# A forgetting-attention and bilinear feed-forward kernel: all operations in a new order around an early first feed-forward piece, reciprocals merged, one more batch masked by GpSimd, fewer idle matmuls

## The chip, the cores and the metric

The kernel runs on one core of a Trainium2 chip. The metric is device time in microseconds (us) of one execution; a kernel's time is the median over its runs. Before the change the median of 3 runs is 394.45 us, from 394.08 to 394.82 us.

TensorE (PE in the profile) does the matmuls, VectorE (DVE), ScalarE (ACT) and GpSimd (POOL) the elementwise work, and SyncE (SP) issues most DMA transfers. Each engine works through its own instructions in the order in which they were written out and waits on semaphores for the others.

## The reference

Eight batches of eight heads, 576 positions, head size 64. The scores carry a decay that is a difference of running sums of log f, the softmax is causal, and a feed-forward layer without a nonlinearity follows: the product of two projections, projected back.

```python
scores = np.matmul(q, k.transpose(0, 1, 3, 2)) / np.sqrt(64)
cum    = np.cumsum(np.log(np.clip(f, 0.0001, 1.0)), axis=-1)
scores = np.where(causal, -1e9, scores + cum[:, :, :, None] - cum[:, :, None, :])
attn   = softmax(scores)                                # row maximum, exp, row sum, division
x      = np.matmul(attn, v).transpose(0, 2, 1, 3).reshape(4608, 512)
out    = ((x @ w_a) * (x @ w_b)) @ w_out                # 512 -> 1536 -> 512
```

## The kernel before, in words

**Attention.** The work is cut into 32 *pairs* t = 4 b + pr: batch b and two of its heads. The 576 queries of a pair make five row blocks i = 0 to 4 (the last has 64 rows), and block i sees the key blocks 0 to i. Per pair, in groups of blocks (1 and 0; 2; 3; 4): `qk_group` or `qk_first` makes the scores in PSUM (operations `qk t.g`, L538, L550); DVE finds the row maxima (`max t.i`, L645, or L673, where the decay is added in the same pass); ACT takes exp with the row sum beside it (`exp t.i`, L700 and L704); DVE takes the reciprocal of the sums (L712 and L714, one per pair and block); POOL scales the rows (`norm t.i`, L725; in batches 0 and 1 partly ACT, L723). The blocks 0 to 2 make part A of the probabilities, 3 and 4 part B. They are transposed, by a DMA of SP's queue (`tr`, L739), in batch 0 and in part of batch 1 by PE (`ptr`, tile psP) with an eviction (`pev`). PE then multiplies with v (`pv`, L768 and L783), and DVE or ACT writes the result into xT (`ev`).

**Masks and decay.** In batch 0 PE adds decay and causal mask to the scores by small matmuls (crow with pick, neg64 with low). In batch 1 (pairs 4 to 7, the set PSPREAD) the decay rows are spread over the partitions by PE (`bm`, tile scd) and evicted (`bc`), and PE still adds the mask. From batch 2 on (the set MASKP, pairs 8 to 31) the decay rows come by DMA, and POOL makes a masked copy of them (`mc`, L630, and `ml`, L637), so that DVE's pass over the scores adds decay and mask together.

**Feed-forward.** The tokens are cut into pieces of 256, 256, 256, 384, 512, 512, 512, 512 and 384, and the last 1024 are done by a Strassen-Winograd scheme (tiles wg, wb, og, ob, om). A piece multiplies with w_a (`psa`), ACT copies it (`acopy`), multiplies with w_b (`psb`), DVE multiplies both (`mul`), and `pso` projects back. A piece can start when `ev` of all four pairs has written its tokens: the first 256 tokens need only blocks 0 and 1 of the pairs 0 to 3. The weights come by DMAs that POOL issues (`ldw`, L509, six `wa`/`wb` pieces ahead of most others): the first 512 columns of w_a and of w_b in two halves each, the other 1024 in two halves each, then w_out in three.

**Idle matmuls.** `wake` (L74, tile wake) multiplies the identity with itself in the start; nothing reads the result. There are 24 such operations of four matmuls.

**The order.** Nothing is scheduled when the kernel is built. Every operation has a number in the order of its construction; ORDER lists all 2480 numbers, CHOICE gives the engine of each operation that may run on several, and SLOTS gives the buffer that each tile takes, in turn. The instructions of each engine, and of the DMA queues that it issues, stand in the sequence of that list.

Of the kernel before, what the change touches and what calls it, by code (L numbers as in the profile page):

```python
# [25 lines left out]
def kernel(  # L26
# [11 lines left out]
    nc = tc.nc  # L38

    B, H, S, D = q.shape  # L40
# [5 lines left out]
    NP = H // 2  # L46
# [58 lines left out]
    def paddings():  # L105
# [36 lines left out]
        PA:012302310231023102310231023102310231;PB:01101010101010101010101010101010;S:0101101001101001101010110  # L142
        0110101010101001010101010101010010011010100101001000100010011011010011010100110101001101010110101010101
        ;a16:0120120120120120120120120120120121021021201201201201021021020210210120120121021021021021021;bc:012
        0120120120120120120120120120;ff:01230123013200031230120131312313102312022101012133203012301230123012301
        2301302132021021230230201230231021301230123012012302131231231021230130230132103120301010312013210321023
        1023023102310321321302130213013210321032103102132132012312312303021021023103120313201302130230123120312
        0302102012120102301310210213023123201321301321320120320312032130213021302301213021303210312303021021320
        130213201302312031203120321032102301;ht:0123456789abcd0123456789abcd0123456789ab01cd2345678a019b23cd456
        8017a29bd345c0168279a34bd015c2;n16:01101001011000101001010101010101;n32:0120102102102102010202121220120  # L150
        110102121101202201201201202120;nv:0101010101;osb:010101010100101010101010101001;qd:01010101010101010101
        0101;sc:01010101010101010101010110100101011000101010110010010101101010101011010101010101010100101011101
        10010101011001010111010101010101010101010101010101;st:01234510324510324510324510324510
# [102 lines left out]
    for lo, hi in ((0, 256), (256, S)):  # L256
        n = hi - lo
# [257 lines left out]
    MASKP = {t for t in range(8, NP * B)}  # L515
# [28 lines left out]
    def qk_group(t, g):  # L544
# [7 lines left out]
        if g == 3 and t in MASKP:  # L552
# [156 lines left out]
    def do_recip(t, i):  # L709
        st = T[("st", t)]  # L710
        if i == 4:
            nc.vector.reciprocal(out=st[:, 28:29], in_=st[:, 18:19])  # L712
        else:
            nc.vector.reciprocal(out=st[:, 20 + 2 * i:22 + 2 * i], in_=st[:, 10 + 2 * i:12 + 2 * i])  # L714
# [106 lines left out]
    def attention(t, base):  # L821
# [75 lines left out]
        direct_ex = {}  # L897
        for g, gi in [(g, groups[g]) for g in ((0, 1, 3, 2) if t in MASKP else (0, 1, 2, 3))]:
            qk, su = qk_of[g], None
            for i in gi:  # L900
# [55 lines left out]
                rc = Op("DVE", 0.16, lambda _, i=i: do_recip(t, i), es, prio=prio(g))  # L956
                st_users.extend(es + [rc])
                for h in range(1 if i == 4 else 2):
                    nm = Op(None, {"POOL": NORM[i]} | ({"ACT": 0.2 + 0.00082 * 128 * (i + 1)} if b in EARLY else {}), lambda e, i=i, h=h: do_norm(e, t, i, h), [rc], prio=prio(g),
                            name=f"norm{t}.{i}")  # L960
                    st_users.append(nm)
                    pu[part].append(nm)
                    norms.setdefault(part, []).append(nm)
                    norm_of.append((i, nm))
# [593 lines left out]
    for n in cuts:  # L1558
# [5 lines left out]
        0 1 29 30 46 2 52 62 5 3 31 37 32 38 33-36 39 40 42 41 53 47 58 4 43 267 262 279 6-9 54 48 10 56 50 44  # L1564
# [161 lines left out]
```

## Time and profile before

| | |
|---|---|
| median of 3 runs | 394.45 us |
| profiled execution, its own time from first to last instruction | 394.4 us |
| PE busy | 381.1 us (97%) |
| DVE busy | 329.1 us (83%) |
| ACT busy | 299.4 us (76%) |
| POOL busy | 281.0 us (71%) |
| granted TensorE clock | 0.999 of full speed |

A row of a timeline has start and length in us, engine, line, operation, output and inputs, shapes, the number of instructions merged into it, and in brackets the idle time ahead and what ended it. A matmul's length contains its way through the array, so consecutive rows overlap; what a matmul takes from the stream is read from start to start. In a table of windows each engine has busy us and, in brackets, instructions.

### The profile page before, as it was taken

What the parts mean: (1) busy time and instruction counts of PE and PEld (TensorE: products, weight loads), DVE (VectorE), ACT (ScalarE), POOL (GpSimd) and SP (SyncE); (2) the same over time, 40 slices, a digit from 0 to 9 for tenths busy, and PEclk for the clock granted to TensorE, in tenths of its full rate; (3) what the DMA queues carried; (4) which work ended last, traced back from release to release, by engine and by line L of the source; (5) the groups of instructions that cost most, each with busy time, mean ns of one, the idle gap of its engine ahead of it and who ended that gap; (6) DMA issues with size and microseconds to landing.
All of it is one profiled execution on the core that took longest, in us unless ns stands there. A gap on an engine that the chain in (4) does not pass through costs nothing.

```text
span 394.4 us, 14909 instructions
## 1 busy us (share of the span) xinstructions
PE 381.1 (97%) x5816; PEld 253.9 (64%) x5816; DVE 329.1 (83%) x1035; ACT 299.4 (76%) x826; POOL 281.0 (71%) x482
## 2 busy tenths in 40 slices
PE   7899999999998999999899999999999999999996
PEld 3557887968765665655555655555555667666796
DVE  7888898998996888788788888757898899987992
ACT  4998999999886878868888588779899672556331
POOL 8689686768867689874899769578976891267600
PEclk9999999999999999999999999999999999999999
DMA  7999999999999999999998999999998898100005
GB/s 121 251 202 170 144 154 223 228 278 275 208 222 215 220 282 247 281 187 277 260 237 255 262 207 229 206 244 263 226 226 195 169 182 178 55 1 2 2 2 214
DMA packets 147190, 76.88 MB, mean 195 GB/s; under 512 B 124336, under 2 KB 128176, under 8 KB 147120
## 3 DMA queue, kind: packets, MB, share of 16 engines
q1 hardware_dynamic: 132824, 68.79, 77.9%
q0 software_dynamic: 14256, 7.08, 14.7%
q8 instruction: 45, 0.74, 0.8%
q14 instruction: 25, 0.20, 0.2%
q10 hardware_dynamic: 40, 0.07, 0.1%
HBM read 52.05 MB, written 9.58 MB: 156 GB/s over the span
## 4 chain that ended last, share of the span: by engine, by line
PE 73%; DMA 11%; DVE 5%; POOL 4%; ACT 3%; issue 2%; ACTq 0%; DVEq 0%; POOLq 0%
PE psa L74 15%; PE psb L74 15%; PE pso L74 13%; PE wg L74 5%; DMA PTA<-PA 5%; PE wb L74 4%; PE sc L550 3%; PE og L74 3%; DMA PTB<-PB 3%; PE pvx L768 3%; PE psT L358 2%; DVE S L673 2%; DMA wb<-in_moe_w_b_dram 2%; POOL PA L725 2%; PE wake L74 2%
## 5 line engine op out<-in xcount | busy, mean ns | idle before, releaser
L673 DVE CUSTOM_DVE_ANT_0 S<-sc,spread 64x576 f32<-64x576 f32 (+4 forms) x232 | 125.5, 561 | 14.5 <-ACT PA L704 4.8
L725 POOL TENSOR_SCALAR PA<-PA,st 128x256 f16<-128x256 f16 (+2 forms) x180 | 85.0, 481 | 9.6 <-DVE st L714 6.0
L74 PE MATMUL psb<-xT,wb 128*64 128x512 f16 (+2 forms) x864 | 88.7, 332 | 0.4 <-DVE ht L1072 0.2
L704 ACT ACTIVATE PA<-S,st 128x256 f16<-128x256 f32 (+2 forms) x168 | 84.1, 503 | 6.4 <-DVE st L673 5.8
L74 PE MATMUL psa<-xT,wa 128*64 128x512 f16 (+2 forms) x864 | 88.9, 333 | 0.0
L74 PE MATMUL pso<-wout,ht 128*64 128x512 f16 x672 | 81.8, 381 | 0.0
L725 POOL TENSOR_SCALAR PB<-PB,st 128x512 f16<-128x512 f16 (+1 forms) x90 | 63.6, 713 | 25.3 <-DVE st L714 8.8
L74 PEld LDWEIGHTS <-wb 128*64 128x64 f16 x960 | 55.9, 110 | 24.9 <-issue 1.8
L74 PEld LDWEIGHTS <-wa 128*64 128x64 f16 x960 | 55.2, 110 | 24.7 <-issue 2.2
L1072 DVE TENSOR_TENSOR ht<-psb,a 128x512 f16<-128x512 f32 (+1 forms) x90 | 57.5, 648 | 7.2 <-PE psb L74 5.1
L288 ACT CAST a<-psa 128x512 f16<-128x512 f32 (+1 forms) x90 | 49.4, 550 | 18.0 <-PE psa L74 15.8
L74 PEld LDWEIGHTS <-ht 128*64 128x64 f16 x696 | 38.3, 110 | 26.8 <-issue 2.2
L704 ACT ACTIVATE PB<-S,st 128x512 f16<-128x512 f32 x56 | 40.2, 720 | 3.2 <-DVE st L673 2.7
L704 ACT ACTIVATION_READ_ACCUMULATOR PA<-S,st 128x1 f32 x168 | 32.1, 191 | 0.0
L630 POOL TENSOR_SCALAR_AFFINE_SELECT spread<-spread 128x768 f32<-128x768 f32 x24 | 20.8, 866 | 14.0 <-DMA spread<-cum_d 13.9
L700 ACT ACTIVATE PB<-S,st 128x576 f16<-128x576 f32 x28 | 21.7, 776 | 10.7 <-DMA PTB<-PB 4.1
L768 PEld LDWEIGHTS <-nv 128*64 128x64 f16 x640 | 21.8, 110 | 8.5 <-DMA PTA<-PA 2.3
L673 DVE CUSTOM_DVE_ANT_1 S<-sc,spread 128x256 f32<-128x256 f32 x48 | 19.7, 419 | 7.5 <-ACT PB L704 1.6
L1273 POOL TENSOR_TENSOR hy<-wu 128x512 f16<-128x512 f32 x9 | 11.6, 1302 | 19.7 <-DVE wu L1273 19.6
L714 DVE RECIPROCAL st<-st 128x2 f32<-128x2 f32 x128 | 18.1, 156 | 7.2 <-ACT PA L704 3.6
L673 DVE DVE_READ_ACCUMULATOR2_ANT st<- 128x1 f32 (+1 forms) x280 | 22.8, 81 | 0.0
L550 PE MATMUL sc<-kT,qT 64*128 64x512 f16 (+4 forms) x144 | 21.0, 326 | 1.2 <-ACT kT L288 0.4
(156 smaller groups left out, 692.8 us busy)
## 6 DMA issues: line engine op xcount, KB each, us to landing
spread<-cum_d SPq DMA_DIRECT2D x24, 576.0 KB, 6.4
q<-in_q_dram SPq DMA_DIRECT2D x14, 576.0 KB, 5.3
k<-in_k_dram SPq DMA_DIRECT2D x14, 576.0 KB, 5.4
out_dram<-osb SPq DMA_DIRECT2D x29, 256.0 KB, 4.0
v<-in_v_dram SPq DMA_DIRECT2D x24, 256.0 KB, 5.8
wout<-in_moe_w_out_dram POOLq DMA_DIRECT2D x3, 512.0 KB, 8.0
nv<-in_v_dram POOLq DMA_DIRECT2D x8, 128.0 KB, 5.1
wa<-in_moe_w_a_dram POOLq DMA_DIRECT2D x2, 512.0 KB, 7.5
```

The source lines that it names most:

```text
L74: nc.tensor.matmul(out=out[r], lhsT=lhsT[:, r], rhs=rhs, **kw)
L288: nc.scalar.copy(out=out_, in_=in_)
L550: nc.tensor.matmul(out=dst, lhsT=lhsT, rhs=rhs, start=start, stop=stop, skip_group_check=True)
L630: nc.gpsimd.affine_select(out=c[:, :, 0:SM].rearrange("p h (j k) -> p h j k", k=128), in_=c[:, :, SM:2 * SM].rearrange("p h (j k) -> p h j ...
L673: nc.vector.tensor_tensor_reduce(out=o, in0=x, in1=y, scale=-1.0, scalar=3e38, op0=ADD, op1=MIN, accum_out=m)
L700: nc.scalar.activation(out=p_blocks(t, 4), in_=T[("s" if direct else "z", t, 4)], func=EXP, bias=st[:, 8:9], scale=sign, accum_out=st[:, 1 ...
L704: nc.scalar.activation(out=p_blocks(t, i)[:, :, h, :], in_=(T[("s", t, i)][:, h, :] if direct else T[("z", t, i)][:, h * n:h * n + n]).rea ...
L714: nc.vector.reciprocal(out=st[:, 20 + 2 * i:22 + 2 * i], in_=st[:, 10 + 2 * i:12 + 2 * i])
L725: VEC[e].tensor_scalar(out=p, in0=p, scalar1=st[:, c:c + 1], scalar2=1.0, op0=MUL, op1=MUL)
L768: nc.tensor.matmul(out=o[HP[h], 128 * i:128 * i + 128], lhsT=vt[:, j, pr + NP * h, :], rhs=pt[:, base_blk[i] + 2 * block_at(t, i, j) + h, ...
L1072: nc.vector.tensor_tensor(out=ht[:, 0:n_], in0=T.pop(("psb", t0, fbs))[:, 0:n_], in1=T.pop(("a16", t0, fbs))[:, 0:n_], op=MUL)
L1273: VEC[e].tensor_tensor(out=out_, in0=x, in1=y, op=op)
```

## The change

ORDER, CHOICE and SLOTS are new throughout; 2386 operations are left of 2480. Beside them four edits:

```diff
-    for n in range(24):
-        o = Op("PE", 0.427, lambda _: wake(2), [o_i], prio=-290, mode="full", name=f"wake{n}")
+    for n in range(10):
+        o = Op("PE", 0.427, lambda _, n=n: wake(2 if n < 6 else 1), [o_i], prio=-290, mode="full", name=f"wake{n}")
...
-    MASKP = {t for t in range(8, NP * B)}
+    MASKP = {t for t in range(4, NP * B)}
...
-        if g == 3 and t in MASKP:
+        if g == 3 and t in MASKP and t not in PSPREAD:
...
-    def do_recip(t, i):
+    RGROUPS = {True: [(0, 1, 2), (3, 4)], False: [(0, 1), (2,), (3, 4)]}
+
+    def do_recip(t, blocks):
         st = T[("st", t)]
-        if i == 4:
-            nc.vector.reciprocal(out=st[:, 28:29], in_=st[:, 18:19])
-        else:
-            nc.vector.reciprocal(out=st[:, 20 + 2 * i:22 + 2 * i], in_=st[:, 10 + 2 * i:12 + 2 * i])
+        c0, c1 = 2 * blocks[0], 9 if blocks[-1] == 4 else 2 * blocks[-1] + 2
+        nc.vector.reciprocal(out=st[:, 20 + c0:20 + c1], in_=st[:, 10 + c0:10 + c1])
...
-                rc = Op("DVE", 0.16, lambda _, i=i: do_recip(t, i), es, prio=prio(g))
+                for blocks in RGROUPS[b not in EARLY]:
+                    if i not in blocks or not all(x in ex_of for x in blocks):
+                        continue
+                    rc = Op("DVE", 0.16, lambda _, blocks=blocks: do_recip(t, blocks), sum((ex_of[x] for x in blocks), []),
```

- 10 idle operations instead of 24: six of four matmuls and four of two, 32 matmuls instead of 96.
- Batch 1's causal mask comes from POOL (four `mc` and four `ml` more) instead of PE (16 mask matmuls fewer for each of four pairs), but for the last 64 rows, which keep PE's mask. `mc` follows both evictions `bc`.
- One reciprocal for the blocks 0, 1 and 2 and one for 3 and 4, from batch 2 on; in the batches 0 and 1 one for 0 and 1, one for 2 and one for 3 and 4. There are 72 instead of 160, and a block's `norm` operations wait for exp of its whole group.
- The new order. Its main turns, by names read off the two lists:

| | before | after |
|---|---|---|
| PE ahead of the first `psa` | `wake` x24, `pt`/`pu` x8, `qk` of pairs 0 to 3 up to qk2.2, `bm` x5, `ptr` x7, `pv` x4 | `wake` x10, `pt`/`pu` x7, the same without qk1.2 and qk2.2, `bm` x3, `ptr` x5, `pv` x4 |
| POOL's `ldw` | the eight of `wa` and `wb` one by one between `norm` operations, the first after four of them, the last behind 21 | one half of the later columns of `wa` ahead of the constants; one half of the first columns of each of `wa` and `wb` after 5 norms; the other halves after 14 norms, with the other late `wa`; both late halves of `wb` further on |
| ACT in the start | blocks 1, 0 and 2 of pair 0, then pair 1, then the others | blocks 1 and 0 of all four pairs, then block 2 of each |
| PE at the end of attention | ... `pso`, pv30, pv31, `pso` x2, then the first Winograd product (wg) | ... pv30, `pso` x3, pv31, then wg x3, wb |
| DVE there | eleven of twelve `ws` (weight differences) done, then `xs` (token sums, L1224) beside the two `pso` | seven `ws` done, three more behind pv31 in the list, then `xs` in the order 0, 1, 3, 2, 0, each on one half of the rows; the first wb on sums needs both halves of `xs` 0 |

The first Winograd products read tokens of batch 7 and so wait for `ev` of pair 31.

More of the change, by code (lines that the diff above doesn't have):

```diff
@@ L147 @@
[L147 to L151, printed above, removed]
@@ L154 @@
+        123456789ab0123456789cd0;n16:01010101001010101110001001010001;n32:012012010120121021120012021201102022
+        0120120120201021020121021;nv:0101010101;osb:010101010011101011001010101101;qd:010101010101010100100101
+        ;sc:01010101010101001010100101100101100100101010101001101010101001010100101010010110100100101010100101
+        10101001010100100010010101100001100101010101010;st:01234501234501234501234051240315
     """
@@ L955, in attention @@
                 su.extend(es)
-                rc = Op("DVE", 0.16, lambda _, i=i: do_recip(t, i), es, prio=prio(g))
[L957 to L964, printed above, removed]
+                st_users.extend(es)
+                ex_of[i] = es
+                for blocks in RGROUPS[b not in EARLY]:
+                    if i not in blocks or not all(x in ex_of for x in blocks):
+                        continue
+                    rc = Op("DVE", 0.16, lambda _, blocks=blocks: do_recip(t, blocks), sum((ex_of[x] for x in blocks), []),
+                            prio=prio(g), name=f"rc{t}.{blocks[0]}")
+                    st_users.append(rc)
+                    for x in blocks:
+                        for h in range(1 if x == 4 else 2):
+                            nm = Op(None, {"POOL": NORM[x]} | ({"ACT": 0.2 + 0.00082 * 128 * (x + 1)} if b in EARLY else {}),
+                                    lambda e, x=x, h=h: do_norm(e, t, x, h), [rc], prio=prio(g), name=f"norm{t}.{x}")
+                            st_users.append(nm)
+                            pu[part_of(t, x)].append(nm)
+                            norms.setdefault(part_of(t, x), []).append(nm)
+                            norm_of.append((x, nm))
         trs, ptu = {}, {}
@@ L1680 @@
+        PPPPPPPDADAAPPPAPPPPDAAAAAAAADDADAAAAAAAAADAADDADDADAAAAADADADAAADAAAAAAADAAAADADDAADAAADAAAAADAAAADDA
+        AAAAADDAADDAADAADDADAAAAAAADDAADAAAADAAAAAAAAAAADAAAAAAAAAAAAAAADADAADA
     """
```

88 lines of the change are left out of this document (58 added, 30 removed), and 146 rows, old and new, of the table ORDER.

## The prediction

> **What bounds the kernel now.** I read the windows by stage first, then PE's timeline up to the first feed-forward piece, then PE's waits. Columns of a window: start and end, length, busy us and instructions of PE, of its weight loads, of DVE, ACT and POOL, then the granted clock.
>
> ```profile
> 0.00:36.00 36.00, 31.18 (x548) 18.34 (x550) 29.67 (x76) 28.32 (x84) 29.75 (x62) 1.00 0.99 189
> ...
> 63.00:90.00 27.00, 26.84 (x546) 21.32 (x544) 24.66 (x89) 26.01 (x69) 20.75 (x36) 1.00 1.16 256
> ```
>
> From 36 us on PE is nearly full, as in the second row, so the end is set by how much PE work is left when it becomes full. The first 36 us are different: PE looks busy, but idle matmuls fill it, and softmax of batch 0 on ACT, DVE and POOL sets the pace. The first useful piece starts where psa stands:
>
> ```profile
> 33.72 0.53 PE L74 MATMUL psP<-ident,PA 128*64 128x128 f16 x12
> 34.06 0.41 PE L74 MATMUL scd<-crow,pick 128*64 128x512 f16 x2
> 34.27 0.36 PE L768 MATMUL pv<-xT,nv 128*64 128x128 f16 x6
> 34.56 0.39 PE L550 MATMUL sc<-kT,qT 64*128 64x512 f16 x2
> ...
> 35.80 1.06 PE L74 MATMUL psa<-xT,wa 128*64 128x256 f16 x16
> ```
>
> Later PE waits little. These are the waits from 60 us on, with sum, times and longest:
>
> ```profile
> PE pvx L768 <- DMA PTA<-PA: 2.0, 4, 0.7
> PE sc L538 <- DVE ht L1072: 1.1, 1, 1.1
> PE sc L74 <- DVE xT L292: 1.0, 1, 1.0
> ```
>
> So the change is worth what it gains ahead of 36 us, plus PE work removed, plus PE waits made or removed later.
>
> **The change part by part.** *Fewer idle matmuls* are worth nothing by themselves: they fill time in which PE has nothing to do, and the order around them decides.
>
> *The early piece.* The new order does blocks 1 and 0 of all four pairs first, so two conditions decide when psa can start: their 14 norms on POOL, and the weights that POOL issues between them. The rows for both, and the time in which wa's parts land after their issue (minimum, median, maximum), which I take for wb too:
>
> ```profile
> 14.03 0.37 POOL L725 TENSOR_SCALAR PA<-PA,st 128x128 f16<-128x128 f16 x1 [2.84 <-DVE st L714]
> ...
> 14.51 1.82 POOL L304 DMA_DIRECT2D nv<-in_v_dram  x2
> ...
> 23.05 0.65 POOL L509 DMA_DIRECT2D wa<-in_moe_w_a_dram  x1
> ...
> 24.34 2.29 POOL L725 TENSOR_SCALAR PA<-PA,st 128x256 f16<-128x256 f16 x5
> ...
> DMA to landing us min/median/max: 5.0/6.5/7.9
> ```
>
> The first norm starts near 14.0 as now: the first exps are no earlier, and POOL has waited 2.84 us by then, which hides the weight DMA put ahead of it. Then come eight norms of 128 columns (0.37 each, 3.0 us), six of 256 (2.29 / 5 = 0.46, 2.8 us), one v issue (1.82 / 2 = 0.9) and two weight issues (1.3): 8.0 us. The second half of wa's first columns is issued at 22.0, wb's 0.65 later. With the median landing wa is there at 28.5 and wb at 29.2, and psa keeps PE for most of the time between. I take 28.5 for the first psa, between 27.0 (fastest landing) and 29.9 (slowest): 7.3 us earlier than 35.80.
>
> Not all of that is gained, because PE work is put behind it: one transpose of queries (pt), two score operations (qk1.2 and qk2.2), two bm and two ptr. A ptr takes 0.34 (33.72 to 34.06), a bm 0.21 (34.06 to 34.27), a late qk of batch 0 1.24 (34.56 to 35.80), a pt at most 0.44:
>
> ```profile
> 43.07 0.44 PE L358 MATMUL psT<-ident,k 64*128 64x64 f16 x18
> ...
> 45.18 1.06 PE L74 MATMUL psb<-xT,wb 128*64 128x256 f16 x16 [0.21 <-DMA wb<-in_moe_w_b_dram]
> ```
>
> Together 0.44 + 2.48 + 0.42 + 0.68 = 4.0 us. Gain: 7.3 - 4.0 = 3.3 us (1.9 to 4.8), if PE then stays as full as now. What speaks for it: ahead of the second piece's first acopy the new ACT list holds one exp, two norms and two evictions less and one eviction more. What speaks against it: a late half of wb is issued only behind a scaling of part B, and the third psb needs it; in the trace that psb comes at 45.18, so there is room for it.
>
> *Batch 1 masked by POOL.* PE loses 16 matmuls for each of four pairs:
>
> ```profile
> 50.36 0.28 PE L550 MATMUL sc<-neg,low 64*128 64x64 f16 x8
> 50.47 0.33 PE L550 MATMUL sc<-kT,qT 64*128 64x384 f16 x2
> 50.64 0.22 PE L550 MATMUL sc<-neg,low 64*128 64x64 f16 x4
> 50.79 1.06 PE L74 MATMUL psb<-xT,wb 128*64 128x256 f16 x16
> ```
>
> Eight take 0.11 to the next start and four 0.15, so a pair's 16 take 0.41; at eight's own rate they take 0.22, since part of the 0.15 is the turn to another operation, which stays. Four pairs: 0.9 to 1.6 us; I take 0.9. Splitting two key runs adds no columns. POOL gets four mc (866 ns) and four ml (404 ns) more, 5.1 us:
>
> ```profile
> L630 POOL TENSOR_SCALAR_AFFINE_SELECT spread<-spread 128x768 f32<-128x768 f32 x24 | 20.8, 866 | 14.0 <-DMA spread<-cum_d 13.9
> ...
> L637 POOL TENSOR_SCALAR_AFFINE_SELECT spread<-spread 128x256 f32<-128x256 f32 x24 | 9.7, 404 | 5.4 <-DVE st L673 5.3
> ```
>
> The same mask by its line (minimum, median and maximum ns):
>
> ```profile
> L630 POOL TENSOR_SCALAR_AFFINE_SELECT spread<-spread x24: 859/865/871, 76.0 to 306.6; 128x768 f32<-128x768 f32 x24
> ```
>
> POOL idles 6.25 us between 63 and 90 alone, and the four pairs spread over it and the stage before; that idle time hides them, and without it they cost up to 5.1 us. The durations of the last row differ by 12 ns while DVE is busy most of the time, so nothing stretches them. (The Trainium skill, SBUF — State Buffer, section SBUF: two separate sides, has a port pair that DVE and GpSimd lock for a whole instruction when DVE reads two SBUF inputs or runs a two-port mode; by that rule a mask could also hold DVE up. The 12 ns show no sign of it at the masks.)
>
> *Merged reciprocals.* 88 of these go, the larger merged ones being a few elements longer:
>
> ```profile
> L714 DVE RECIPROCAL st<-st 128x2 f32<-128x2 f32 x128 | 18.1, 156 | 7.2 <-ACT PA L704 3.6
> ```
>
> DVE is not the bound, so this counts only where PE waits for DVE, 1.1 and 1.0 us above. A pair has three fewer, at most 3 x 0.156 = 0.47 us: those waits shrink by 0 to 0.9. I take 0.5. The other side, later norms, is a rival below.
>
> *The turn to Winograd.* Now two pso stand between pv31 and the first wg. In the timelines, ACT's ev of the pairs 30 and 31:
>
> ```profile
> 333.74 1.35 ACT L288 CAST xT<-pvx 128x576 f16<-128x576 f32 x2 [0.99 <-PE pvx L783]
> ```
>
> DVE's xs:
>
> ```profile
> 335.13 1.68 DVE L1224 TENSOR_TENSOR xT<-xT,xT 128x512 f16<-128x512 f16 x4
> ```
>
> PE's two pso and the first wg:
>
> ```profile
> 334.23 1.92 PE L74 MATMUL pso<-wout,ht 128*64 128x512 f16 x16
> 335.96 1.06 PE L74 MATMUL wg<-xT,wa 128*64 128x512 f16 x8
> ```
>
> In the new list wg follows pv31 directly and has to wait for ev31, 0.7 us. Then three wg and one wb (16 matmuls, 1.73 us as for the two pso) cover the five xs up to the second half of xs 0 (5 x 0.42 = 2.1): 0.4 us are left. Cost 1.1 us; 0 if PE is behind DVE and ACT in another way, 2.5 if the three ws ahead of xs are late too (twice an xs's columns, so by estimate 0.7 each, 2.1 less the 0.7 of ev31).
>
> *Everything else moved.* PE's other work, DVE's passes and the DMAs are the same in number, and only their places differ. The waits of 4.1 us shown above can vanish or double; without a row that says which, I take no difference, from -4 to +4.
>
> Sum against the profiled 394.4 us: -3.3 - 0.9 - 0.5 + 1.1 = -3.6, so 390.8 us. The span is within 0.1 us of the median of the runs, so nothing is added.
>
> **The rivals.** *The gain is absorbed* (chance 0.14). Between 63 and 90 ACT is busy for 26.0 of 27 us and DVE for 24.7. If these, not PE, set the pace up to the third piece, an earlier start only makes PE wait. DVE's 16 fewer reciprocals in the batches 0 and 1 then are the whole gain, 16 x 0.156 = 2.5 us, less 1.1 at Winograd: 393.0 us. Against it: PE has only 0.16 us idle there.
>
> *Slower: A's transposes come late* (0.14). From batch 2 on, norms of the blocks 1 and 0 (two of 0.37, two of 0.46, 1.7 us) can start now while exp of block 2 still runs; merged, all six norms start after it, so part A leaves POOL up to 1.7 us later, 24 times. Place: pv's wait for PTA. From issue to landing a transpose takes:
>
> ```profile
> DMA to landing us min/median/max: 3.7/4.9/7.8
> ```
>
> Four of 24 pairs already have no time left (the waits of 2.0 us). Should those four and one more be exposed, that is 8.5 us: 399.3. It decides from three exposures, since 2 x 1.7 is still less than 3.6. For it: the new list has three pairs (16, 25 and 31) whose last norm of A stands within 2.5 us of PE work of its pv, the old list none. Against it: the exps still stand 20 us and more of PE work ahead of pv in both lists, and POOL may run ahead of its place.
>
> *The clock falls* (0.08). The first 20 idle matmuls take nearly twice as long each as the next eight, whose 1.06 us also hold one way through the array:
>
> ```profile
> 2.80 4.48 PE L74 MATMUL wake<-ident 128*64 128x512 f16 x20 [2.80 <-POOL ident masks.py:199]
> 8.30 1.06 PE L74 MATMUL wake<-ident 128*64 128x512 f16 x8
> ```
>
> About 0.22 us each against 0.13: PE starts at half speed for those 4.5 us. With 64 idle matmuls fewer, PE has more holes up to 28 us. If it is slow again when psa starts, it loses half of another 4.5 us: 390.8 + 2.2 = 393.0. Against it: in the new list qk, pt and ten idle operations still stand in each stretch. (The Trainium skill, TensorE: Matmul & The Clock Gate, Part 1, has the clock halved after an idle window of about 3.4 us; by that rule only a hole of that length would do it. The slow first 4.48 us agree; no row here shows a fall back.)
>
> *More than forecast* (0.14). The later waits of 4.1 us vanish with the new places and psa starts at 27.0: 390.8 - 4.1 - 1.5 + 0.5 (already counted) = 385.7 us.
>
> **How the numbers follow.** My forecast, 390.8, has 0.50. Its own bounds are 387.5 (first psa at 27.0, masks 1.6, nothing at Winograd) and 394.1 (first psa at 29.9, nothing from DVE, 2.5 at Winograd). For 8 in 10 I go down to 384.5, a us past the best rival, and up to 396.5, a third of the way from the upper bound to the late transposes, whose price the unknown waits of 4 us would also reach. About 0.2% (0.8 us) is what a measurement of this kernel can tell from no change. Faster by more: the forecast with nearly all of its 0.50 (0.47), more than forecast (0.14), the clock (0.07) and half of the absorbed case (0.06), 0.74. Slower: most of the late transposes (0.13) and a rest, 0.15. Within 0.2%: 0.11.
>
> **What would show it.** Right: the first psa between 27 and 30 us, its psb directly behind; PE in 36 to 90 as full as now; no sc<-neg,low of 64x64 in batch 1 but at the last rows; a PE wait of about 0.7 us for xT right after pv31. Wrong: a first psa past 31; waits of pvx for PTA above 5 us in sum (late transposes); idle matmuls or qk past 10 us at twice their length (clock); PE idle in 36 to 90 by more than 2 us (absorbed).

## The result

| | before | after |
|---|---|---|
| time, median of 4 runs | 394.63 us (394.08 to 397.78) | 409.36 us (408.80 to 409.69) |
| ratio, 95% interval | 1 | 1.040 (1.036 to 1.044) |
| span of the profiled execution | 394.4 us | 407.4 us |
| PE, DVE, ACT, POOL busy | 97%, 83%, 76%, 71% | 93%, 80%, 73%, 71% |
| granted clock | 0.999 | 0.987 |

The change makes the kernel 4% slower; 390.8 us was forecast. The two spans differ by 13.0 us, the times by 14.7: the profiled execution of the kernel before is one of its longer ones (in the sets below its spans go from 389.9 to 395.2 us). Where the 13.0 us go is read in views of the changed kernel. First PE's timeline at the early piece:

```profile
29.13 1.04 PE L74 MATMUL psa<-xT,wa 128*64 128x256 f16 x16
30.00 1.04 PE L74 MATMUL psb<-xT,wb 128*64 128x256 f16 x16
...
38.83 0.89 PE L74 MATMUL psP<-ident,PB 128*64 128x128 f16 x26
43.59 1.90 PE L74 MATMUL psb<-xT,wb 128*64 128x256 f16 x16 [3.86 <-DMA wb<-in_moe_w_b_dram]
```

The first psa stands at 29.13 (forecast 28.5) and its psb directly behind. But the third psb, at 45.18 before, comes at 43.59 only, and PE stands still for 3.86 us ahead of it. The chain of waits has the cause in one row, start and length of a transfer:

```profile
32.91 10.54 DMA wb<-in_moe_w_b_dram
```

The second late half of wb is issued at 32.91 (37.17 before) and is 10.54 us on its way (7.87 before). It stands behind the first late half, which was issued at 28.7 and itself took 10.1 us. PE's waits of the whole execution, sum, times and longest:

```profile
PE wb L74 <- DVE wu L1280: 6.8, 6, 1.6
PE psb L74 <- DMA wb<-in_moe_w_b_dram: 3.9, 1, 3.9
PE wake L74 <- POOL ident masks.py:199: 2.8, 1, 2.8
PE pvx L768 <- DMA PTA<-PA: 2.3, 2, 1.8
PE psT L358 <- DMA q<-in_q_dram: 1.6, 1, 1.6
PE psb L74 <- ACT osb L288: 1.6, 1, 1.6
```

The first row is new: six waits of the Winograd stage's product into wb for a DVE sum in wu. (In that stage wb, wg and wu are tiles of products and sums; wb in a DMA row is the weight w_b.) Two tables of windows give the weight of both places, before and then after (start and end, length, busy us of PE, PEld, DVE, ACT, POOL, clock):

```profile
36.00:60.00 24.00, 23.79 (x545) 20.34 (x543) 21.70 (x76) 23.06 (x69) 17.58 (x25) 1.00 1.31 151
60.00:100.00 40.00, 39.84 (x800) 32.62 (x798) 36.20 (x129) 37.79 (x99) 30.50 (x53) 1.00 1.10 256
100.00:340.00 240.00, 235.53 (x3300) 143.19 (x3298) 199.91 (x690) 188.06 (x535) 179.72 (x325) 1.00 1.05 225
...
340.00:390.00 50.00, 50.00 (x628) 38.94 (x624) 41.06 (x68) 21.78 (x43) 23.47 (x18) 1.00 0.07 26
```

```profile
36.00:60.00 24.00, 20.03 (x440) 16.41 (x438) 18.64 (x57) 18.81 (x53) 18.00 (x25) 0.93 1.20 201
...
340.00:390.00 50.00, 43.07 (x447) 26.25 (x442) 39.53 (x63) 21.86 (x41) 23.43 (x18) 1.00 0.03 9
```

PE loses 3.8 us between 36 and 60 and 6.9 us between 340 and 390. The last stage, from the first Winograd product (335.96 before, 340.21 after) to the end, takes 58.4 us before and 67.2 after: 8.8 of the 13.0 lie in it and 4.2 ahead of it. The early lead is gone by the first out-product. The tile wout has its first and last start, before and then after:

```profile
L74 PE MATMUL pso<-wout,ht x48: 379/379/382, 54.3 to 65.3; 128*64 128x512 f16 x48
```

```profile
L74 PE MATMUL pso<-wout,ht x48: 379/379/403, 59.3 to 66.0; 128*64 128x512 f16 x48
```

### The profile page after: what moved, and what is told of

Its sections match the earlier page's. It is cut to its first block, busy times and chain, and to the rows that moved or that the text cites. A ratio compares the mean times of both kernels' runs of the same rounds, so it can differ in the third digit from the quotient of the medians.

```text
span 407.4 us, 14568 instructions
## 1 busy us (share of the span) xinstructions
PE 378.7 (93%) x5704; PEld 252.5 (62%) x5704; DVE 324.9 (80%) x948; ACT 297.4 (73%) x821; POOL 290.1 (71%) x494
## 4 chain that ended last, share of the span: by engine, by line
PE 53%; POOL 17%; DMA 14%; issue 6%; DVE 5%; ACT 3%; SPq 1%; POOLq 0%; ACTq 0%; DVEq 0%
PE psb L74 10%; PE psa L74 10%; PE pso L74 10%; POOL PA L725 6%; POOL PB L725 5%; PE wg L74 4%; DMA PTB<-PB 4%; PE wb L74 4%; DMA q<-in_q_dram 3%; DMA out_dram<-osb 3%; PE sc L550 3%; PE og L74 3%; DMA wb<-in_moe_w_b_dram 3%; DVE S L673 2%; PE pvx L768 2%
## 5 line engine op out<-in xcount | busy, mean ns | idle before, releaser
L673 DVE CUSTOM_DVE_ANT_0 S<-sc,spread 64x576 f32<-64x576 f32 (+3 forms) x224 | 121.7, 567 | 14.3 <-ACT PA L704 3.7
L725 POOL TENSOR_SCALAR PA<-PA,st 128x128 f16<-128x128 f16 (+2 forms) x182 | 86.4, 486 | 10.5 <-DVE st L714 8.2
L725 POOL TENSOR_SCALAR PB<-PB,st 128x512 f16<-128x512 f16 (+1 forms) x92 | 65.9, 724 | 22.6 <-DVE st L714 12.6
L74 PE MATMUL pso<-wout,ht 128*64 128x512 f16 x672 | 80.4, 380 | 0.4 <-DVE ht L1079 0.3
L74 PEld LDWEIGHTS <-wa 128*64 128x64 f16 x960 | 56.7, 110 | 24.5 <-issue 2.1
L673 DVE CUSTOM_DVE_ANT_1 S<-sc,spread 128x256 f32<-128x256 f32 x56 | 22.8, 419 | 12.7 <-issue 4.9
L630 POOL TENSOR_SCALAR_AFFINE_SELECT spread<-spread 128x768 f32<-128x768 f32 x28 | 24.3, 868 | 3.7 <-DMA spread<-cum_d 3.6
L637 POOL TENSOR_SCALAR_AFFINE_SELECT spread<-spread 128x256 f32<-128x256 f32 x28 | 11.3, 405 | 16.4 <-DVE st L673 16.0
L714 DVE RECIPROCAL st<-st 128x6 f32<-128x6 f32 (+3 forms) x72 | 12.4, 176 | 12.9 <-ACT PB L704 6.9
L550 PE MATMUL sc<-kT,qT 64*128 64x512 f16 (+5 forms) x160 | 20.9, 321 | 1.6 <-ACT PA L704 1.1
```

Source lines behind the costliest of these rows:

```text
L74: nc.tensor.matmul(out=out[r], lhsT=lhsT[:, r], rhs=rhs, **kw)
L550: nc.tensor.matmul(out=dst, lhsT=lhsT, rhs=rhs, start=start, stop=stop, skip_group_check=True)
L630: nc.gpsimd.affine_select(out=c[:, :, 0:SM].rearrange("p h (j k) -> p h j k", k=128), in_=c[:, :, SM:2 * SM].rearrange("p h (j k) -> p h j ...
L637: nc.gpsimd.affine_select(out=x, in_=x, compare_op=mybir.AluOpType.is_ge, fill=NEGBIG, base=0, pattern=[[0, 2], [-1, 128]], channel_multip ...
L673: nc.vector.tensor_tensor_reduce(out=o, in0=x, in1=y, scale=-1.0, scalar=3e38, op0=ADD, op1=MIN, accum_out=m)
L714: nc.vector.reciprocal(out=st[:, 20 + c0:20 + c1], in_=st[:, 10 + c0:10 + c1])
```

## The experiments

Times of one set share runs of the kernel before; its median lay between 393.1 and 394.2 in the five sets, so ratios to it (95% interval) are what is compared; a gain or loss in us is a difference of two ratios, times that median. "Changed" is the kernel with the change, at 1.040 (1.036 to 1.044).

### The late weights, and the last stage

**e1_wb_early**, on the changed kernel:

```diff
 POOL: ... ldwa(61) ldwb(62)
+      ldwb(64) ldwb(63)
       ca1q0 norm ... 
-      ldwb(64) ... norm x4 ... ldwb(63)
```

> The changed kernel with one thing moved: the two late halves of wb are issued by POOL directly behind wb's and wout-free first columns, after the fourteenth norm, instead of behind four and six further norms (issued near 24.5 and 25.2 us instead of 28.7 and 32.9). Theory A (late weights cost the start): the third psb no longer waits 3.86 us for wb, the clock no longer falls near 44 us, and the time falls by 4 to 6 us, to 403.5-405.5. Rival (weights land 8 to 10 us after issue because the DMA engines are full there, and what is moved ahead only pushes the norms behind it): psb still waits 2 us or norms of part B come later by 1.3 us, and the time falls by less than 2 us, to 407.4 or more.

Measured: 404.25 us, 1.028 (1.021 to 1.034), clear of the changed kernel's interval: 1.2% or 4.8 us of the loss. Its waits of PE have this for wb, and its windows this for 36 to 60:

```profile
PE psb L74 <- DMA wb<-in_moe_w_b_dram: 0.5, 1, 0.5
```

```profile
36.00:60.00 24.00, 22.54 (x504) 17.93 (x502) 22.32 (x72) 22.90 (x67) 20.62 (x29) 1.00 1.33 215
```

Theory A holds: 2.5 of the 3.8 us come back, and the last stage starts at 336.4 us instead of 340.2; its length stays 67.2 us. The rival has a point too. The transfers now take up to 14.8 us from issue to landing, so being issued 6.5 us earlier brings the third psb only 2.2 us forward (41.38 in this kernel's timeline).

**e2_win**, on the changed kernel; the same instructions from the first wg on, in the order and on the engines of before. The first products on PE and their sums on DVE, with the number of the block of hidden columns behind the dot:

```diff
-PE:  wm1.0 wm1.1 wm1.2 wm2.1 wm5.1 wm6.1 wm6.0 wm2.0 wm5.0 wm7.1 wm7.0 wm3.1 wm3.0 wm6.2 wm4.1 wm4.0
-DVE: snap1.2 c11.1 c22.0 c11.0 c12.0 c12.1 h2.0 h2.1
+PE:  wm1.0 wm1.1 wm2.0 wm5.0 wm2.1 wm5.1 wm6.0 wm1.2 wm1.3 wm3.0 wm7.0 wm6.2 wm6.1 wm2.2 wm3.1 wm4.0
+DVE: c11.0 c11.1 c12.0 c22.0 snap6.1 c12.1 h2.0
```

> The changed kernel with the last stage's instructions (from the first Winograd product on) in the order and on the engines of the kernel before; all ahead of it stays. Theory B (the third product stands directly behind the DVE sum it needs, so PE and DVE wait for each other in turn): PE's 6.8 us of waits of wb for DVE wu go to below 1, and the time falls by 6 to 8 us, to 401.5-403.5. Rival (the stage is late because of what comes into it - weight sums, input sums and evictions left over from before - not because of its own order): the waits move to other operands, and the time falls by less than 2 us.

Measured: 402.91 us, 1.026 (1.018 to 1.033): 5.8 us. From 340 us on its waits of PE are these alone:

```profile
PE wg L74 <- DVE osb L292: 1.1, 1, 1.1
PE wb L74 <- DVE xT L1231: 0.7, 1, 0.7
PE wg L74 <- ACT wu L288: 0.2, 1, 0.2
```

The six waits for wu are gone, and the stage takes 61.3 us instead of 67.2, so theory B holds: the order of this stage alone makes them. The two longer waits left stand near the turn to the stage: one for a token sum of DVE in xT, one for a bank (a part of PSUM) out of which DVE has yet to copy an out-product (osb).

**e15_wm3**, on e1_wb_early:

```diff
-PE: ... wm7.3 wm3.3 wm1.6 ...
+PE: ... wm7.3 wm1.6 wm3.3 ...      # nine of the twelve wm3
```

> The changed kernel with wb's late halves issued early (404.25) and nine of the last stage's twelve third products (wm3) exchanged with the PE product right behind them; all else as in the change. Theory B in its narrow form (wm3 stands too close behind the DVE sum it needs): each moved product has 0.43 us more to wait for its sum, so 9 x 0.43 = 3.9 us at most, 2 to 4 us faster, 400.3-402.3. Rival (the two banks of wb make the chain c11, wm3, c12, next wm2 the pace, whatever stands between): the wait moves to c12 and to wm2, within 1 us of 404.25.

Measured: 405.29 us, 1.031 (1.024 to 1.038), no faster than e1_wb_early. The wait that it aims at:

```profile
PE wb L74 <- DVE wu L1280: 4.7, 5, 1.3
```

2.1 of the 6.8 us go and the stage takes 66.2 us instead of 67.2, too little to be told by time. One more place per product doesn't mend the stage; the old order of both engines does (e2_win).

**e13_wb_win**, both edits:

```diff
+POOL as in e1_wb_early
+PE, DVE, ACT from the first wg on as in e2_win
```

> The changed kernel with wb's late halves issued early and the last stage in the order and on the engines of before; no idle matmul added. If the two edits add up: 409.4 - 5.1 - 6.5 = 397.8 (396.5-399). If one takes the other's place (PE, earlier at 60 us, only waits for softmax later): 400 or more.

Measured: 402.56 us (398.37 to 403.18), 1.019 (1.012 to 1.026). The two add up to 2.1% where 2.7% would be the sum; the intervals allow both readings, the median doesn't reach the 399 expected. By its trace the stage takes 61.4 us but starts at 339.3, 2.9 us later than in e1_wb_early, though all ahead of it stands in the same order: PE waits 2.2 us for wout there, 0.3 in e1_wb_early. So one trace each can't price what lies ahead of the stage to better than some 3 us.

**e14_turn**, on e13_wb_win:

```diff
 PE:  ... pv30 pso pso
-     pso(2109) pso(2110) pv31 wm1
+     pv31 pso(2109) pso(2110) wm1
-DVE: ... ocopy ...
+ACT: ... snap1 snap1 ocopy ...
```

> The kernel above, with the last two out-product operations of PE (1.7 us) put behind the last attention product, so that they cover its eviction and the input sums, and the last eviction of these out-products on ACT, as the kernel before has both. The prediction's fifth step put this stall at 1.1 us (0 to 2.5), and in the trace of the last stage's own undoing PE waits 0.69 for xT and 1.12 for a bank there: 1.5 to 2 us faster than the kernel above, about 396. Rival (the last attention product itself waits for its transposes, which the out-products ahead of it covered): within 0.7 us of the kernel above.

Measured: 401.28 us, 1.017 (1.010 to 1.023); no difference from e13_wb_win can be told by time. By one trace each, 340 to 390 us, first e13_wb_win and then e14_turn, it does what was expected of it:

```profile
340.00:390.00 50.00, 47.89 (x544) 34.67 (x542) 43.48 (x73) 23.44 (x46) 23.46 (x18) 1.00 0.02 7
```

```profile
340.00:390.00 50.00, 49.70 (x598) 37.43 (x596) 42.33 (x69) 23.09 (x46) 23.49 (x18) 1.00 0.05 18
```

With it the last stage is nearly as full as before and takes 59.1 us (58.4 before). By the runs 1.7% or 6.5 us stay. The trace, of an execution of 398.61 us, shows less: the last stage starts at 337.8, 1.8 us later than before, and is 0.7 us longer. Most of what stays then lies ahead of the last stage, but no trace shows all of it.

### The clock

**e3_wake**, on the changed kernel; **e5_wake_alone**, on the kernel before:

```diff
-wake(2 if n < 6 else 1)
+wake({6: 4, 4: 8}.get(n, 2 if n < 6 else 1))
 PE: ... pt0q0 pt0k0
+    wake6
     pt0q1
+    wake4
     pu0q0 qk0.0 ...
```

> The changed kernel with more idle matmuls near the start: one idle step of 16 matmuls goes between the first two groups of transposes (6.8-8.3 us) and one of 32 behind the third (8.6-10.4 us), so that PE never rests there; 48 matmuls more, no other order changed. Theory C (the early fall of the clock delays the scores of batch 0 and all behind them): clock 1.00 in 10-20 us instead of 0.68, first norm near 14.5 instead of 15.79, first psa near 28, and the time falls by 1 to 1.5 us, to 407.9-408.4. Rival (the scores wait for the queries' transfer, which lands at 10.33, and for POOL, whatever the clock): clock 1.00, first norm not before 15.4, and the time stays within 0.5 us of 409.4.

```diff
-    for n in range(24):   ... wake(2)
+    for n in range(10):   ... wake(2 if n < 6 else 1)
```

> The kernel before with the change's idle matmuls alone: 32 instead of 96, the first 24 in the places of the first idle steps, the last 8 in the places of four later ones; all other instructions in the order of before. Theory D (the prediction's first step: idle matmuls are worth nothing by themselves): within 0.5 us of before. Rival C (they hold the clock where PE has little to do, and the scores of batch 0 wait for PE): the clock falls below 0.9 somewhere in 8-36 us and the time rises by 1 to 4 us.

Measured: e3_wake 409.63 us, 1.043 (1.036 to 1.050), no gain; e5_wake_alone 394.74 us, 1.003 (1.000 to 1.007). The clock did fall. Windows of the changed kernel, of e3_wake and of e5_wake_alone (third number from the right is the clock):

```profile
8.00:10.00 2.00, 0.48 (x36) 0.37 (x36) 1.51 (x4) 1.98 (x4) 1.83 (x8) 0.88 1.11 168
10.00:12.00 2.00, 1.63 (x36) 1.35 (x38) 0.76 (x1) 0.00 (x0) 1.78 (x8) 0.50 1.10 193
12.00:14.00 2.00, 1.79 (x66) 1.68 (x66) 1.78 (x3) 1.31 (x5) 0.88 (x2) 0.50 1.10 263
```

```profile
10.00:12.00 2.00, 1.94 (x34) 1.02 (x29) 0.00 (x0) 0.93 (x2) 1.82 (x7) 1.00 1.11 209
12.00:14.00 2.00, 1.64 (x81) 1.54 (x78) 1.89 (x4) 0.81 (x2) 0.53 (x1) 1.00 1.09 265
```

```profile
10.00:20.00 10.00, 7.79 (x140) 4.65 (x139) 7.96 (x15) 9.37 (x39) 6.47 (x11) 0.70 1.16 273
20.00:30.00 10.00, 7.75 (x114) 5.64 (x114) 8.65 (x22) 8.82 (x29) 8.62 (x17) 0.67 0.93 178
```

With the clock full up to 16 us in e3_wake the first norm still starts at 15.87 us (15.79 in the changed kernel), so the scores wait for something else: theory C falls for the changed order, and its rival, that the queries' transfer and POOL set the pace, fits. The edit doesn't remove all of the slow time, though. By the clock records of the traces it is 6.83 us in the changed kernel, from 9.52, and still 3.41 us in e3_wake, from 17.76. In the old order half speed lasts some 13 of 20 us (3.0 and 3.3 us of clock missing, twice that at half speed) and the price is 1.3 us (0 to 2.7). That interval holds both the 0.5 us of theory D and the 1 to 4 us of its rival, so between these two e5_wake_alone doesn't decide.

**e4_all3**, the edits of e1_wb_early, e2_win and e3_wake:

```diff
+POOL as in e1_wb_early; last stage as in e2_win; wake as in e3_wake
```

> The three edits of the kernels above together. If the three theories hold and add up: 409.4 - 5 - 7 - 1.2 = 396.2 (394.5-398), about the kernel before; if the early piece is worth its forecast 3.3 us once its weights are there, 392-394.5. If waits only move from one place to the next, 400 or more.

Measured: 400.64 us, 1.020 (1.012 to 1.027), the same as e13_wb_win without the idle matmuls.

### The early piece

**e8_late_piece**, on e1_wb_early:

```diff
-PE: ... ptr1A1 psa psb ptr0A1 psa ptr2A1 qk1.2 pt1q0 psb psa ptr0B ptr0B bm5 qk2.2 ptr3A1 ptr1B ptr1B psb ...
+PE: ... ptr1A1 ptr0A1 ptr2A1 qk1.2 pt1q0 ptr0B ptr0B bm5 qk2.2 ptr3A1 psa ptr1B ptr1B psb psa psb psa psb ...
```

> The changed kernel with wb's late halves issued early (404.25 us on this kind of comparison) and the first two pairs of gate and value products (and the third gate product) moved back behind the score operations, transposes and evictions of batch 0 that they had overtaken, to where the kernel before has them. If the early piece is worth what the prediction's second step says: 3 us slower, about 407. Rival E (softmax of batch 0 sets the pace up to 60 us on ACT, DVE and POOL, and the piece is only taken out of 36-60 us, where PE then runs dry): within 1 us of 404.25, or faster.

Measured: 411.52 us, 1.045 (1.039 to 1.050) against 1.028: 6.6 us slower. The early piece is worth more than the 3.3 us forecast in this order, and rival E falls. Its windows say why more:

```profile
28.00:36.00 8.00, 6.07 (x88) 3.96 (x90) 5.21 (x9) 4.06 (x10) 7.22 (x12) 0.62 1.13 242
36.00:60.00 24.00, 20.43 (x444) 17.69 (x442) 17.14 (x48) 17.59 (x45) 15.33 (x21) 0.99 1.06 197
```

Without the piece PE rests, the clock falls to 0.62, and all engines do less in both windows than in e1_wb_early, whose row for 36 to 60 stands above and whose other one is:

```profile
28.00:36.00 8.00, 7.71 (x170) 6.44 (x172) 5.98 (x11) 5.22 (x12) 7.42 (x12) 1.00 1.07 220
```

**e9_front**, on e1_wb_early, and **e16_turn_front**, the same on e14_turn:

```diff
-PE:  pt0q1 pu0q0 qk0.0 ...      DVE: pe0q1 max0.1 max0.0      ACT: pe0k1 exp0.1 exp0.0 ...
+PE:  pt0q1 qk0.0 pu0q0 ...      DVE: max0.1 max0.0 pe0q1      ACT: exp0.1 exp0.0 ... pe0k1
```

> The changed kernel with wb's late halves issued early (404.25 us) and the first scores put ahead again: PE's qk0.0 ahead of the transposes of the second half of the queries, whose transfer lands at 10.33, DVE's first two maxima ahead of the eviction of these transposes, ACT's first four exponentials ahead of an eviction of keys. Theory F (softmax of batch 0 sets the pace from its first exponential on): first exponential near 11.8 us instead of 13.22, first norm near 14.5 instead of 15.79, and the time falls by 1 to 1.5 us, to about 403. Rival (POOL's weight issues and norms set the pace, so an earlier first norm only makes POOL wait later): within 0.5 us of 404.25.

> The kernel with the turn mended (wb early, last stage as before, out-products behind the last attention product), and the first scores put ahead of the late queries' transposes. Theory F: first norm near 14.5 us instead of 15.8 and 1 to 1.5 us faster than the kernel without it. Rival: within 0.5 us of it, as POOL and the transposes behind set the pace.

Measured: 408.02 us, 1.035 (1.028 to 1.041) against 1.028; and 401.13 us, 1.019 (1.013 to 1.026) against 1.017. Not faster. In e16_turn_front ACT is through with the first four exponentials at 12.78, but DVE's timeline goes on like this:

```profile
10.99 0.76 DVE L290 TENSOR_SCALAR qT<-psT 128x576 f16<-128x576 f16 x1
13.46 0.76 DVE L292 COPY kT<-psT 128x576 f16<-128x576 f16 x1 [1.72 <-PE psT L358]
14.44 1.02 DVE L645 TENSOR_REDUCE st<-sc 128x2 f32<-128x512 f32 x2 [0.22 <-PE sc L550]
15.49 0.18 DVE L714 RECIPROCAL st<-st 128x4 f32<-128x4 f32 x1
```

The first norm waits for that reciprocal, and the reciprocal stands behind an eviction of keys and another pair's maxima. It starts at 15.78, against 15.79 in the changed kernel and 15.21 in e14_turn: theory F fails because the reciprocal's place on DVE, not the exponential, sets it.

### The masks and the reciprocals

**e6_mask_alone**, on the kernel before:

```diff
-    MASKP = {t for t in range(8, NP * B)}
+    MASKP = {t for t in range(4, NP * B)}
-        if g == 3 and t in MASKP:
+        if g == 3 and t in MASKP and t not in PSPREAD:
 DVE, t = 4..7:
-     max t.3 x2, max t.4 x2
+     max t.4 x2, max t.3 x2     (exp, rc and norm likewise; ml on POOL behind max t.4)
```

> The kernel before with batch 1's masks on GpSimd alone: 64 small matmuls less on PE, four mc and four ml more on POOL, and for each pair of batch 1 block 4 ahead of block 3 on DVE, ACT and POOL; all else in the order of before. The prediction's third step: -0.9 us (-1.6 to -0.6). Rival (POOL paces the stretch where batch 1 is prepared, and block 3 now waits for a mask that waits for block 4): 0 to +3 us, with PE idle more in 35-70 us.

Measured: 404.16 us, 1.025 (1.020 to 1.030): 10 us slower. PE's windows and POOL's wait of ml, sum, times and longest:

```profile
36.00:60.00 24.00, 23.37 (x510) 19.65 (x508) 20.86 (x74) 22.03 (x66) 19.32 (x27) 1.00 1.34 151
60.00:100.00 40.00, 32.49 (x612) 24.82 (x610) 29.50 (x104) 31.34 (x79) 25.68 (x45) 1.00 0.73 189
```

```profile
POOL spread L637 <- DVE st L673: 20.2, 9, 6.4
```

Up to 60 us nothing is lost. Then POOL stands in ml for maxima of block 4, up to 6.4 us at a time (5.3 us in sum before), with norms behind it, and PE runs dry: 32.49 busy of 40, against 39.84 before (the row is above). The price is that of the wait, and of the exchange of blocks 3 and 4 that comes with it, in a list not laid out for them.

**e10_no_mask**, on e1_wb_early, takes the masks back to PE:

```diff
-    MASKP = {t for t in range(4, NP * B)}
+    MASKP = {t for t in range(8, NP * B)}
 POOL:
-     mc4 ml4 mc5 ml5 mc6 ml6 mc7 ml7
```

> The changed kernel with wb's late halves issued early (404.25 us) and batch 1 masked on PE again: 64 small matmuls more on PE, four mc and four ml less on POOL, order else unchanged. The prediction's third step: 0.9 us slower, about 405.2. Rival G (POOL's masks cost more than the matmuls they save, since POOL sets the pace up to 60 us and waits for maxima with norms queued behind): 1 to 3 us faster, 401-403.

Measured: 409.12 us, 1.041 (1.037 to 1.045) against 1.028: 5 us slower. In the new order, which is laid out for them, the masks pay, and more than the matmuls' 0.9 us; 36 to 60 us are less full (PE 20.36 of 24 busy, against 22.54), with third-psb waits of 1.6 us for wb again. Rival G falls.

**e7_recip_alone**, on the kernel before:

```diff
+    RGROUPS = {True: [(0, 1, 2), (3, 4)], False: [(0, 1), (2,), (3, 4)]}
 DVE:  rc t.0 ... rc t.1 ... rc t.2
-      (three)
+      (one, in the place of the last)
 POOL: norms that stood ahead of it go right behind it
```

> The kernel before with merged reciprocals alone: 88 fewer on DVE, each merged one in the place of the last of its group, and the norms that stood ahead of it put right behind it; all else in the order of before. The prediction's fourth step: -0.5 us. Rival (the norms of a group's first blocks now wait for its last exponentials, so batch 0's first norms and all transposes behind norms come later): +1 to +4 us, the first norm at 14.8 us or later instead of 14.03.

Measured: 419.46 us, 1.065 (1.061 to 1.069): 26 us slower. Its waits of POOL for the reciprocal:

```profile
POOL PA L725 <- DVE st L714: 20.8, 11, 4.4
POOL PB L725 <- DVE st L714: 20.7, 11, 4.6
```

6.0 and 8.8 us are the same two in the kernel before. So in the old order the merging, placed like this, makes the norms wait as its rival said, and costs far more than the 1 to 4 us that the rival gave.

**e11_no_merge**, on e1_wb_early:

```diff
-    RGROUPS = {True: [(0, 1, 2), (3, 4)], False: [(0, 1), (2,), (3, 4)]}
+    RGROUPS = {True: [(0,), (1,), (2,), (3,), (4,)], False: [(0,), (1,), (2,), (3,), (4,)]}
 DVE: each rc right behind the last exp of its block in the list
```

> The changed kernel with wb's late halves issued early (404.25 us) and separate reciprocals, each right behind the last exponential of its own block; norms and all else in the order of the change. The prediction's fourth step: 0.5 us slower, about 404.8. Rival H (merging makes the norms of a group's first blocks wait for its last exponentials, which costs more than 88 reciprocals on DVE): 1 to 4 us faster, 400-403, with POOL's waits of PA and PB for the reciprocal (20 us) at least halved.

Measured: 462.77 us, 1.178 (1.173 to 1.183), 59 us slower than e1_wb_early; neither theory had that. Its waits of DVE:

```profile
DVE st L714 <- ACT PA L704: 50.1, 65, 1.9
DVE st L714 <- ACT PB L704: 20.3, 22, 1.9
DVE st L714 <- ACT PB L700: 14.2, 15, 1.7
```

85 us of DVE standing in reciprocals for ACT. So the experiment measured its own placement, and rival H stays untested: DVE works its list in order, and "right behind the exp" in the list is too early on DVE by as much as ACT is behind. What separate reciprocals would cost in a good place of the new order isn't known.

**e12_best1**, the edits of e1_wb_early, e9_front, e11_no_merge and e2_win:

```diff
+all four
```

> Four edits of the changed kernel together: wb's late halves issued early, the first scores put ahead, separate reciprocals, and the last stage in the order of before. If they add up (5, 1, 0 to 3 and 6.5 us off 409.4): 394-397, near the kernel before; 391 if the early piece is worth its 3.3 us beyond that.

Measured: 459.26 us, 1.167 (1.162 to 1.172): it holds the edit of e11_no_merge, which alone costs as much, and nothing can be read beyond that.

### The weights behind the weights

**e17_wout** and **e18_wout_wake**, on e14_turn. In that kernel the first out-product waits 1.5 us for wout, whose parts are issued back to back; in the tile's view:

```profile
L509 POOL DMA_DIRECT2D wout<-in_moe_w_out_dram x3: 747/760/768, 41.1 to 42.6; - x3
...
DMA to landing us min/median/max: 7.3/11.9/15.2
```

```diff
 POOL: lds0v4 mc4 lds0v2
+      ldwo ldwo ldwo
       norm1.3 ca1q1 lds0v3
-      ... ldwo ... ldwo ... ldwo
```

> e14_turn with the three issues of wout's weights moved ahead on POOL, from 41.1 us to near 36, ahead of one scaling of batch 0's part B. If late weights are once more what takes the gain: the 1.5 us wait of the first out-products goes, PE is about 1 us ahead of the kernel before at 60 us, and the time falls by 1 to 2 us from e14_turn (398.6-402.9 in single runs, with its median 401.3), to about 399.5. Rival (2.3 us of issues ahead of a scaling delay part B's transposes as much): within 0.7 us of e14_turn.

> e17_wout with 48 idle matmuls more in 6.8-10.4 us, as in e3_wake. If the clock in the first 30 us takes part of the gain: mean clock 0.995 or more and 1 to 3 us faster than e17_wout. If softmax sets the pace there (as e3_wake's 409.63 against 409.36 says): within 0.7 us.

Measured: 411.00 us, 1.044 (1.040 to 1.048), and 411.95 us, 1.047 (1.043 to 1.051): 11 us slower than e14_turn, and idle matmuls change nothing that shows. One row of PE's waits tells where:

```profile
PE pv L783 <- DMA nv<-in_v_dram: 8.6, 1, 8.6
```

POOL now issues lds0v3, 128 KB of v, behind wout's 1.5 MB. It lands 13.0 us after its issue, where v's other parts of that stretch take 5.0 and 5.8, and pv waits. Neither theory had looked at what is queued behind.

No kernel of these beats the kernel before.

## Why the prediction was wrong

- **Idle matmuls, worth nothing by themselves: about right.** Leaving them out costs 1.3 us (0 to 2.7) in the old order; putting 48 of the 64 back gains nothing that shows in the new one. The clock rival had its sign, matmuls past 10 us at twice their length, but not its place: it had psa slow, and by 18 us the clock was back.
- **The early piece: the start right, the condition behind it wrong.** First psa at 29.13 for 28.5, psb behind it, and the piece is worth 6.6 us in e8_late_piece. What failed is the sentence on the third psb: "in the trace that psb comes at 45.18, so there is room for it". The change that was being priced moves that psb forward itself, to about 39.7 (the end of the work ahead of it in the timeline), while the weight moved only from 37.17 to 32.91. And the flight time of 5.0 to 7.9 us, taken from parts issued one at a time, was 10.54, behind a half that took 10.1. By the prediction's own bound, 32.9 + 7.9 = 40.8, the wait would have been 1 us; the flight made it 3.9. "If PE then stays as full as now" fell with it: 20.03 of 24 us for 23.79.
- **Masks on POOL, -0.9 us: the sign right in the new order, the size wrong in both.** Undone there it costs 5 us; alone in the old order it costs 10. The step set 5.1 us of POOL work against POOL's idle time. It left out that ml waits for DVE's maxima of block 4, and that the norms stand in POOL's queue behind it.
- **Merged reciprocals, -0.5 us: priced as instructions, and they are waits.** DVE's reciprocals fell from 160 to 72 as forecast. Put into the old order as in e7_recip_alone, the merging costs 26 us, in POOL's waits for them. The rival "A's transposes come late" had the mechanism; its sign, pvx waiting for PTA above 5 us in sum, did not come in the changed kernel (2.3 us); that the new order is laid out for it is likely, but not shown. What they cost there stays open.
- **The turn to Winograd, +1.1 us: too dear, by a wait that isn't there.** From 340 us on no row of PE's waits is for xT. The first wg starts before ev of pair 31 has even begun:

```profile
340.21 1.49 PE L74 MATMUL wg<-xT,wa 128*64 128x512 f16 x12
340.45 0.64 ACT L288 CAST xT<-pvx 128x576 f16<-128x576 f32 x1 [3.27 <-PE pvx L783]
```

  In the code this first product reads features 0 to 255, which ev of the pairs 28 and 29 writes; only the next one, into wb, reads those of the pairs 30 and 31. So the sentence in "The change" that the first products wait for ev of pair 31 holds for wb, not for wg, and the three wg cover that eviction and the token sums. A stall was seen only where e2_win and e13_wb_win put the old order behind the new turn (0.7 and 1.1 us), and e14_turn's mending can't be told by time.
- **Everything else moved, 0 (-4 to +4): wrong by 8.8 us in the last stage alone**, 6.8 of them PE's six waits. That stage had no waits before, so the 4.1 us of waits by which I bounded this term had nothing of it. A chain between two engines that stand in each other's way at each block, PE's product into wb, DVE's sum into wu, PE's next product, was not followed in the two lists.
- **The rival "gain is absorbed"** has its sign, PE idle in 36 to 90 us above 2 us, but not by its cause: late weights, not ACT and DVE.
- **Two workings.** The span of 394.4 us was set beside a median of other executions; an execution's time is about 1.7 us longer than its span. And a third of the way from 394.1 to 399.3 is 395.8, not the 396.5 of the range; the measured time is far past both.

Shown by the runs: 4.8 us from wb's late halves, 5.8 us from the order of the last stage, 8.3 us when both are mended. So about half of the loss (4.0%, 15.8 us) is traced to these two. Left over the kernel before are 6.5 to 7.6 us. The one trace of e14_turn has PE 1.7 us less busy than before in 36 to 60 us and 1.9 in 100 to 340:

```profile
36.00:60.00 24.00, 22.09 (x502) 17.58 (x498) 21.84 (x71) 23.07 (x68) 20.33 (x28) 1.00 1.30 210
...
100.00:340.00 240.00, 233.63 (x3276) 144.63 (x3274) 190.43 (x614) 189.50 (x538) 183.20 (x330) 1.00 1.02 223
```

Most of the first is the 1.5 us for wout, and mending that failed; why the middle is less full in the new order, and where the rest of the 6.5 us lies, stays open.

## What to carry to other kernels

When a step is moved ahead, recompute for the new place every date that it is checked against: the weight that had room for the old place of its user has none for the new one. A merged or added wait in an in-order queue is priced by who stands behind it, not by its instruction. In a list laid out as a whole, parts of a change can't be taken out and priced one by one: taken alone, or taken back, most of them cost 5 to 26 us, whatever they are worth in the list made for them.

## What the runs showed of the hardware

- **The clock fell without a long rest.** In e3_wake PE works on scores and idle matmuls, with rests of 1.22 and 0.74 us, in these two windows, and from 18 to 20 us the granted clock is 0.50:

```profile
14.00:16.00 2.00, 0.78 (x29) 0.75 (x25) 1.86 (x5) 2.00 (x11) 0.14 (x1) 1.00 1.07 357
16.00:18.00 2.00, 1.21 (x30) 0.80 (x24) 1.94 (x5) 1.83 (x11) 1.91 (x4) 0.94 1.19 337
```

  The changed kernel has the same from 8 to 10 us, 0.48 of 2 us busy, rests of 0.69 and 1.63 us, then 0.50 up to 16 us; but all its work there is transposes, so it alone would not show that work with short rests is too little. The Trainium skill, TensorE: Matmul & The Clock Gate, Part 1, has the clock halve after an idle window of some 3.4 us; in e3_wake the clock falls at 17.76 us, after 3.41 us in which PE was busy for 1.45. So the prediction's reading, that only a hole of that length would do it, does not hold here. The hole of 3.86 us ahead of the third psb fits the page: 0.62 in the 4 us behind it. In the clock records of these traces, ahead of the last 4 us, every stretch at half clock lasts 3.41 us or a whole multiple of it.
- **POOL's transfers land in turn.** Three parts of 512 KB issued back to back landed 7.3, 11.9 and 15.2 us after issue, in that order, and the 128 KB behind them in e17_wout 13.0 us after its own. The Trainium skill, DMA: Bandwidth & Descriptors, Queues, rings and completion order, says for the queues of SP and ACT that each DMA engine takes descriptors in ring order; POOL's transfers here look the same. So here a flight time taken from transfers issued some us apart was too short for one with more ahead of it: 5.0 to 7.9 us against 10.54.
- **About 1.7 us lie outside the span** in nearly every timed execution here (409.14 and 407.4; 393.32 and 391.6 of the kernel before), up to 2.6 in a few (399.32 and 396.7). The prediction added nothing for it.
